# Attention's stages, the doubled global outputs and two casts issued at other places of a two-layer kernel

## The chip, the cores and the metric

One core of a Trainium2 chip runs the kernel. The metric is device time of one execution in microseconds (us); several runs are taken and their median is given. TensorE (PE) multiplies, VectorE (DVE), ScalarE (ACT) and GpSimd (POOL) do the elementwise work, SyncE (SP) issues every DMA here. Each engine runs its instructions in the order in which they were issued.

## The reference

Attention over 4 batches of 8 heads of 64, with 512 local and 32 global rows per batch. A local row attends to the global rows and to a window of 32 to each side; a global row attends to everything. The 2176 output rows of width 512 then go through two feed-forward layers (512 to 2048 to 512), all in float32:

```
s_g = scale * np.matmul(q_g, k_all.transpose(0, 1, 3, 2))
out_g = np.matmul(sm(s_g), v_all)
...
s_ll = np.where(mask, s_ll, -1000000000.0)
s_l = np.concatenate([s_lg, s_ll], axis=-1)
a_l = sm(s_l)
out_l = np.matmul(a_l, np.concatenate([v_g, v_l], axis=2))
...
h = x @ w_in
g = h * np.clip(h + 3.0, 0.0, 6.0) / 6.0          # first layer
g = np.where(h > 0.0, h, np.exp(np.minimum(h, 0.0)) - 1.0)   # second layer
(g @ w_out).astype(np.float32)
```

## The kernel before, in words

The rows are 17 tiles of 128: tiles 0 to 15 are local rows (four per batch), the last holds all the global rows. They are grouped into chunks 0 to 4 of 4, 3, 3, 3 and 4 tiles (`CHUNKS`). A chunk runs the first layer in 16 steps, one per block of 128 of the 2048 hidden columns (`f`). A matmul in float32 is done as three in a reduced format, of high and low parts (`xh`/`xl`, `gh`/`gl`), by `mm3`.

A step of the main loop issues, in this order: `up` (12 matmuls into `h`, then at once on ACT and DVE: `g` on ACT, `g` on DVE, `gh` on ACT), part 0's other work, `gl` on DVE, half of `down` (into `acc`) of the step two before, part 1's other work, the other half of `down`, part 2's other work. So a **place** is one of the three parts of a step; I write 5.2 for part 2 of step 5. Between parts 0 and 1 and between 1 and 2 PE has half a down step, between part 2 and the next step's part 0 a whole up.

While chunk 1 runs, attention of tiles 7 to 9 (chunk 2's) and of global blocks G0 to G2 is woven in; beside chunk 2 tiles 10 to 12 and G3 to G5, beside chunk 3 tiles 13 to 15, G6, G7 and the turning of the global outputs. (Chunk 0 has an order written out by hand, and tiles 4 to 6 are in it.) A local tile has four stages (`Local.stages`): scores **S** (64 small matmuls into two PSUM banks, then softmax on DVE and ACT, and the load of the next tile's q and k), **T** (8 transposes into two banks, two copies `PT` on ACT), values **O** (64 small matmuls into two banks, normalising on DVE, the load of the next v) and **XT** (4 transposes into one bank, then `x1h` on ACT and `x1l` on DVE, which read it: `split`). A global block has **SG**, **TG**, **OG** with `PG`, `PTG`, `xg` in the same roles. All of these share the two banks tagged `att`. At the end `turned_global` doubles four of the global outputs (`xgg`, a DVE copy of `xg`), transposes them (**XTG**) and splits the result; it runs twice.

The table `place, step` gives each stage a position, `during` stretches the positions of a chunk over 44 of its 48 places. Beside this `prepare`, a generator, splits the second layer's weights into high and low parts in eight passes and stores them to DRAM (`wd`). Each `yield` names the earliest place and what the next piece costs DVE and ACT; `Pace.step`, called behind each part's work, lets a piece go when its place has come and the work estimated for that engine stays under `ROOM`. Its pieces are `first` (L164), `second` (L167), `third` (L170 and L173), `high` (L179, a cast on ACT) and `low` (L183, on DVE).

Of the kernel before, what the change touches and what calls it, by code (L numbers as in the profile page):

```python
# [10 lines left out]
F32 = mybir.dt.float32  # L11
# [7 lines left out]
B, H, SL, SG, D = 4, 8, 512, 32, 64  # L19
# [4 lines left out]
P = 128  # L24
# [32 lines left out]
REBIAS = 2.0 ** -112  # L57


ROOM, FETCH, STORE = 2.25, 3, 4  # L60


def _tiles():
# [5 lines left out]
def tile_kernel(ctx, tc, qkW, vW, qkG, vN, vG, masks, w1, w2, out):  # L69
    nc = tc.nc  # L70
    pool = ctx.enter_context(tc.tile_pool(name="sb", bufs=1))
# [5 lines left out]
    NC = len(CHUNKS)  # L77
# [5 lines left out]
    xg = pool.tile([P, 2 * B, D], F32, name="xg")  # L83
    banks = {"acc": 4, "h": 2, "att": 2}

    def bank(shape, name, tag):
        return ps.tile(shape, F32, name=name, tag=tag, bufs=banks[tag])
# [65 lines left out]
    def prepare():  # L153

        def load(p, i, part, tag):
            raw = pool.tile([P, DM, 2], I32, name=f"raw1_{p}_{i}_{part}", tag=tag, bufs=1)
            src = w2[2 * p + i].bitcast(I32)[:, part * 2 * DM : (part + 1) * 2 * DM]
            nc.sync.dma_start(raw.rearrange("p c w -> p (c w)"), src)  # L160
            return raw

        def first(w, raw):
            nc.scalar.activation(w.bitcast(F32), raw[:, :, 1].bitcast(F32), AF.Copy, scale=REBIAS)  # L164

        def second(w):
            nc.vector.tensor_single_scalar(w, w, 3, op=ALU.logical_shift_left)  # L167

        def third(w, raw):
            nc.vector.scalar_tensor_tensor(  # L170
                w, raw[:, :, 1], -0x80000000, w, op0=ALU.bitwise_and, op1=ALU.bitwise_or
            )
            nc.vector.scalar_tensor_tensor(  # L173
                w, raw[:, :, 0], 29, w, op0=ALU.logical_shift_right, op1=ALU.bitwise_or
            )

        def high(src, n, name, tag):
            t = pool.tile([P, n, 2, DM // n], F32R, name=name, tag=tag, bufs=1)
            nc.scalar.copy(t[:, :, 0], src)  # L179
            return t  # L180

        def low(t, src):
            nc.vector.tensor_sub(t[:, :, 1], src, t[:, :, 0].bitcast(F32))  # L183

        def out(t, p, at):
            nc.sync.dma_start(wd[p][:, at * DM : at * DM + 2 * DM], t.bitcast(F32).rearrange("p n w k -> p (n w k)"))

        shaped = lambda w, n: w.bitcast(F32).rearrange("p (n k) -> p n k", n=n)
        A, B_, W, X = "f0", "f2", "f1", "f3"
        ra, rb = load(0, 0, 0, A), load(0, 1, 0, B_)  # L190
        ta = tb = pace.now
        for p in range(NF // 2):
            yield ta + FETCH, 0, 0.6
            w = pool.tile([P, 2, DM], I32, name=f"wi{p}", tag=W, bufs=1)
            wa, wb = w[:, 0], w[:, 1]
            first(wa, ra)
            yield pace.now + 1, 0.4, 0
            second(wa)
            yield 0, 1.4, 0
            third(wa, ra)  # L200
            yield tb + FETCH, 0, 0.6
            first(wb, rb)
            yield pace.now + 1, 0.4, 0.6
            ha = high(shaped(wa, 2), 2, f"ha{p}", A)
            second(wb)
            yield 0, 1.4, 0
            third(wb, rb)
            yield 0, 0.7, 0.6
            low(ha, shaped(wa, 2))
            la = pace.now  # L210
            hb = high(shaped(wb, 2), 2, f"hb{p}", B_)
            yield pace.now + 1, 0.7, 0
            low(hb, shaped(wb, 2))
            lb = pace.now
            yield 0, 0.8, 0
            sf = pool.tile([P, 4, 2 * P], F32, name=f"sf{p}", tag=X, bufs=1)
            half = lambda v, k: v.bitcast(F32)[:, 2 * P * k : 2 * P * k + 2 * P]
            nc.vector.tensor_add(sf[:, 2], half(wb, 0), half(wb, 1))
            nc.vector.tensor_sub(sf[:, 0], sf[:, 2], half(wa, 0))
            yield la + 2, 0, 0  # L220
            out(ha, p, 0)
            ta = pace.now
            yield 0, 0.8, 0
            nc.vector.tensor_sub(sf[:, 1], half(wa, 0), half(wb, 0))
            nc.vector.tensor_sub(sf[:, 3], half(wa, 1), sf[:, 0])
            tw = pace.now
            yield lb + 2, 0, 0
            out(hb, p, 2)
            tb = pace.now
            yield tw + 2, 0, 0  # L230
            oa = load(p, 0, 1, W)
            tw = pace.now
            yield ta + STORE, 0, 0.6
            s1 = high(sf[:, :2], 2, f"sa{p}", A)
            yield pace.now + 1, 0.7, 0
            low(s1, sf[:, :2])
            la = pace.now
            yield tb + STORE, 0, 0.6
            s2 = high(sf[:, 2:], 2, f"sb{p}", B_)
            yield pace.now + 1, 0.7, 0  # L240
            low(s2, sf[:, 2:])
            lb = pace.now
            yield la + 2, 0, 0
            out(s1, p, 8)
            ta = pace.now
            yield tw + FETCH, 0, 0.6
            w = pool.tile([P, 2, DM], I32, name=f"wo{p}", tag=X, bufs=1)
            wa, wb = w[:, 0], w[:, 1]
            first(wa, oa)
            yield lb + 2, 0, 0  # L250
            out(s2, p, 10)
            tb = pace.now
            yield 0, 0.4, 0
            second(wa)
            yield 0, 1.4, 0
            third(wa, oa)
            yield pace.now + 2, 0, 0
            ob = load(p, 1, 1, W)
            tw = pace.now
            yield ta + STORE, 0, 0.6  # L260
            ha = high(shaped(wa, 1), 1, f"oa{p}", A)
            yield pace.now + 1, 0.7, 0
            low(ha, shaped(wa, 1))
            la = pace.now
            yield tw + FETCH, 0, 0.6
            first(wb, ob)
            yield pace.now + 1, 0.4, 0
            second(wb)
            yield la + 2, 0, 0
            out(ha, p, 4)  # L270
            ta = pace.now
            yield 0, 1.4, 0
            third(wb, ob)
            tw = pace.now
            yield tb + STORE, 0, 0.6
            hb = high(shaped(wb, 1), 1, f"ob{p}", B_)
            yield pace.now + 1, 0.7, 0
            low(hb, shaped(wb, 1))
            lb = pace.now
            yield tw + 2, 0, 0  # L280
            if p + 1 < NF // 2:
                ra = load(p + 1, 0, 0, W)
            tw = pace.now
            yield lb + 2, 0, 0
            out(hb, p, 6)
            pace.done = p + 1
            yield ta + STORE, 0, 0
            if p + 1 < NF // 2:
                rb = load(p + 1, 1, 0, A)
            ta, tb = tw, pace.now  # L290
            A, B_, W, X = W, A, X, B_
# [25 lines left out]
    pace = Pace()  # L317
# [156 lines left out]
    class Global:  # L474
# [61 lines left out]
        def stages(self, nxt):  # L536
# [9 lines left out]

            return list(zip((first, self.transposed, third), ((1.0, 0.6), (0, 0.8), (0.9, 0))))

    def turned_global(hb):

        (xh, xl), c0 = x_of(len(tiles) - 1)
        xp = bank([P, 2, 2, 2, 2, SG], f"XTG{hb}", "att")
        twice = pool.tile([P, 4, 2, D], F32, name=f"xgg{hb}", tag="ev", bufs=4)
        nc.vector.tensor_copy(twice, xg[:, 4 * hb : 4 * hb + 4].unsqueeze(2).to_broadcast([P, 4, 2, D]))
        for i in range(4):
            transpose(
                xp[:, i // 2, i % 2].rearrange("p a r q -> p (a r q)"),
                twice[:, i].rearrange("p u d -> p (u d)"),
            )
        for par in range(2):  # L560
            r = slice(par * D, par * D + D)
            for b in range(2):
                cs = slice(c0 + (2 * hb + b) * SG, c0 + (2 * hb + b) * SG + SG)
                src = xp[r, b, :, :, par, :].rearrange("p h a q -> p (h a) q")
                nc.scalar.copy(xh[r, :, cs], src)
                nc.vector.tensor_sub(xl[r, :, cs], src, xh[r, :, cs].bitcast(F32))
# [338 lines left out]
    todo = {c: [] for c in range(NC)}  # L905
# [5 lines left out]
    at = {c: 0 for c in range(NC)}  # L911
    for (c, job), (_, nxt) in zip(jobs, jobs[1:] + [(None, None)]):
        if c is not None:
            place, step = ((0, 3, 5, 7), 9) if isinstance(job, Local) else ((0, 3, 5), 6)
            todo[c] += [(at[c] + x, st) for x, st in zip(place, job.stages(nxt=nxt))]
            at[c] += step
    todo[NC - 2] += [(at[NC - 2] + 3 + 2 * i, (lambda i=i: turned_global(i), (0.6, 0.6))) for i in range(2)]
    todo = {c: sorted(v, key=lambda x: x[0]) for c, v in todo.items()}

    def during(c, i):  # L920
# [170 lines left out]
```

## Time and profile before

| | us |
|---|---|
| median of 3 runs (864.95 to 866.28) | 864.99 |
| the profiled execution | 864.55 |
| its span | 862.8 |
| PE busy, 97% | 841.0 |
| DVE busy, 60% | 516.3 |
| ACT busy, 50% | 429.5 |

The span is the profiled stretch from the first to the last instruction; the execution's own time is a little longer. Busy counts modelled ends of pipelined matmuls, so two matmuls overlap in it. In the program's order chunk 1's first up begins at about 136 us, chunk 4's at 407 us.

### The profile page before, as it was taken

How to read it: one execution, taken by the hardware profiler on the slowest of the kernel's cores; microseconds unless marked ns; L12 is line 12 of the kernel's file. 1: busy time of each engine (PE TensorE's matmuls, PEld its weight loads, DVE VectorE, ACT ScalarE, POOL GpSimd, SP SyncE). 2: the span in 40 equal slices, each digit the busy share in tenths (PEclk: the TensorE clock that was granted, in tenths of full speed). 3: DMA queues.
4: the chain of work that ended last, by engine and by line, in shares of the span. 5: the costliest groups of instructions: out<-in, count | busy, mean ns of one | idle time of the engine just before them, and what ended most of it. 6: DMA issues, size and time to landing. Idle time of an engine off the chain costs nothing.

```text
span 862.8 us, 15804 instructions
## 1 busy us (share of the span) xinstructions
PE 841.0 (97%) x6424; PEld 727.1 (84%) x6424; DVE 516.3 (60%) x1125; ACT 429.5 (50%) x835; POOL 4.4 (1%) x8
## 2 busy tenths in 40 slices
PE   8899999999999999998999999999999999999997
PEld 7677778898988899887888889998998888888886
DVE  5788984666565556664655557444456665445443
ACT  6577655454544455543433346454445664444441
POOL 0000000000000000000000000000000000000000
PEclk9999999999999999999999999999999999999999
DMA  9958213656674765563589783946852656444102
GB/s 370 418 210 327 84 52 108 229 180 196 235 258 136 236 230 201 196 201 117 190 296 330 271 315 142 385 172 265 344 187 84 258 208 255 147 147 147 49 1 98
DMA packets 37657, 178.43 MB, mean 207 GB/s; under 512 B 4304, under 2 KB 6224, under 8 KB 25680
## 3 DMA queue, kind: packets, MB, share of 16 engines
q1 hardware_dynamic: 37584, 177.42, 56.9%
q8 instruction: 50, 0.82, 0.4%
q14 instruction: 23, 0.19, 0.1%
HBM read 143.33 MB, written 34.08 MB: 206 GB/s over the span
## 4 chain that ended last, share of the span: by engine, by line
PE 84%; DVE 7%; DMA 4%; ACT 3%; issue 2%; SPq 0%; ACTq 0%; DVEq 0%
PE acc L574 30%; PE h L574 22%; PE ua L574 9%; PE yt L574 9%; PE ub L574 7%; DMA v<-in_vW 1%; PE O L413 1%; PE S L381 1%; PE T L90 1%; DVE f L134 1%; DVE g L601 1%; DVE f L137 1%; DMA raw<-in_w 1%; DVE w L148 1%; DMA qk<-in_qkW 1%
## 5 line engine op out<-in xcount | busy, mean ns | idle before, releaser
L574 PE MATMUL acc<-gh,w 128*128 128x384 f32 (+1 forms) x640 | 199.5, 367 | 0.0
L574 PE MATMUL h<-x1h,w 128*128 128x384 f32 (+1 forms) x640 | 195.7, 367 | 1.6 <-DVE w L148 1.5
L574 PEld LDWEIGHTS h<-x1h,w 128*128 128x128 f32 x640 | 118.5, 189 | 20.1 <-issue 5.3
L574 PEld LDWEIGHTS acc<-gh,w 128*128 128x128 f32 x640 | 119.1, 189 | 13.4 <-issue 0.6
L574 PE MATMUL acc<-gl,w 128*128 128x384 f32 (+1 forms) x320 | 115.6, 361 | 0.8 <-DVE gl L608 0.8
L574 PE MATMUL h<-x1l,w 128*128 128x384 f32 (+1 forms) x320 | 115.5, 361 | 0.2 <-DVE x1l L445 0.2
L601 DVE SCALAR_TENSOR_TENSOR g<-g,h 128x384 f32<-128x384 f32 (+1 forms) x80 | 48.6, 607 | 110.4 <-ACT g L600 110.2
L600 ACT ACTIVATE g<-h,half 128x384 f32<-128x384 f32 (+1 forms) x80 | 49.8, 622 | 93.0 <-PE h L574 92.9
L606 ACT CAST gh<-g 128x384 fp32r<-128x384 f32 (+1 forms) x96 | 52.8, 550 | 77.0 <-DVE g L601 64.9
L574 PE MATMUL ua<-xs,ws 128*128 128x384 f32 (+1 forms) x384 | 88.0, 364 | 0.0
L574 PEld LDWEIGHTS ua<-xs,ws 128*128 128x128 f32 x384 | 70.4, 188 | 10.7 <-ACT s L835 0.3
L608 DVE TENSOR_TENSOR gl<-g,gh 128x384 fp32r<-128x384 f32 (+1 forms) x96 | 57.4, 599 | 24.6 <-ACT gh L606 24.1
L574 PEld LDWEIGHTS acc<-gl,w 128*128 128x128 f32 x320 | 60.4, 189 | 6.5 <-DVE gl L608 1.2
L574 PE MATMUL ub<-xs,ws 128*128 128x384 f32 (+1 forms) x288 | 65.7, 363 | 0.0
L574 PEld LDWEIGHTS h<-x1l,w 128*128 128x128 f32 x320 | 60.4, 189 | 6.1 <-DVE x1l L445 0.5
L574 PEld LDWEIGHTS ub<-xs,ws 128*128 128x128 f32 x288 | 52.7, 188 | 7.0
L877 DVE TENSOR_TENSOR y<-yt,y 128x512 f32<-128x512 f32 x49 | 33.8, 690 | 36.0 <-PE yt L574 35.5
L792 ACT ACTIVATE e<-c 128x384 f32<-128x384 f32 (+1 forms) x48 | 27.8, 580 | 45.8 <-DVE c L828 15.8
L574 PE MATMUL acc<-ws,gg_h 128*128 128x512 f32 x160 | 49.9, 393 | 0.0
L574 PE MATMUL yt<-ws,gg_h 128*128 128x512 f32 x160 | 49.9, 393 | 0.0
L795 DVE SCALAR_TENSOR_TENSOR e<-e,c 128x384 f32<-128x384 f32 (+1 forms) x48 | 30.0, 624 | 23.9 <-ACT e L793 23.3
L793 ACT ACTIVATE e<-e 128x384 f32<-128x384 f32 (+1 forms) x64 | 37.1, 579 | 2.0
(202 smaller groups left out, 1260.2 us busy)
## 6 DMA issues: line engine op xcount, KB each, us to landing
ws<-wd SPq DMA_DIRECT2D x48, 1024.0 KB, 5.4
raw<-in_w SPq DMA_DIRECT2D x16, 1024.0 KB, 11.7
raw<-in_w SPq DMA_DIRECT2D x32, 512.0 KB, 5.4
v<-in_vW SPq DMA_DIRECT2D x13, 1040.0 KB, 6.6
qk<-in_qkW SPq DMA_DIRECT2D x15, 704.0 KB, 6.0
qkG<-in_qkG SPq DMA_DIRECT2D x8, 608.0 KB, 4.6
wd<-ha SPq DMA_DIRECT2D x8, 512.0 KB, 4.8
wd<-hb SPq DMA_DIRECT2D x8, 512.0 KB, 4.8
```

What stands on the lines that cost most here:

```text
L90: nc.tensor.transpose(o, i, ident)
L134: nc.vector.scalar_tensor_tensor(w, self.high[:, s], -0x80000000, w, op0=ALU.bitwise_and, op1=ALU.bitwise_or)
L137: nc.vector.scalar_tensor_tensor(w, self.low[:, s], 29, w, op0=ALU.logical_shift_right, op1=ALU.bitwise_or)
L574: nc.tensor.matmul(o, a, b, start=first and i == 0, stop=last and i == len(pairs) - 1, skip_group_check=more)
L600: nc.scalar.activation(g, hp, AF.Relu, scale=1.0 / 6.0, bias=half)
L601: nc.vector.scalar_tensor_tensor(g, g, 1.0, hp, op0=ALU.min, op1=ALU.mult)
L606: nc.scalar.copy(gh, g)
L608: return lambda: nc.vector.tensor_sub(gl, g, gh.bitcast(F32))
L792: nc.scalar.activation(e, h, AF.Relu, scale=-1.0)
L793: nc.scalar.activation(e, e, AF.Exp, scale=-1.0)
L795: 1, lambda: nc.vector.scalar_tensor_tensor(e, e, -1.0, h, op0=ALU.add, op1=ALU.max)
L877: nc.vector.tensor_add(y, o, y)
```

## The change

Seven edits in the part that orders the work; each instruction stays as it is.

```diff
-ROOM, FETCH, STORE = 2.25, 3, 4
+ROOM, FETCH, STORE = 2.4, 3, 4
...
             third(wb, rb)
-            yield 0, 0.7, 0.6
+            yield pace.now + 1, 0.7, 0.6
             low(ha, shaped(wa, 2))
             la = pace.now
             hb = high(shaped(wb, 2), 2, f"hb{p}", B_)
...
             tw = pace.now
-            yield tb + STORE, 0, 0.6
+            yield max(tb + STORE, tw + 1), 0, 0.6
             hb = high(shaped(wb, 1), 1, f"ob{p}", B_)
...
+    xgg = {}
+
+    def doubled(hb):
+        xgg[hb] = pool.tile([P, 4, 2, D], F32, name=f"xgg{hb}", tag="ev", bufs=4)
+        nc.vector.tensor_copy(xgg[hb], xg[:, 4 * hb : 4 * hb + 4].unsqueeze(2).to_broadcast([P, 4, 2, D]))
+
...
-        xp = bank([P, 2, 2, 2, 2, SG], f"XTG{hb}", "att")
-        twice = pool.tile([P, 4, 2, D], F32, name=f"xgg{hb}", tag="ev", bufs=4)
-        nc.vector.tensor_copy(twice, xg[:, 4 * hb : 4 * hb + 4].unsqueeze(2).to_broadcast([P, 4, 2, D]))
+        xp, twice = bank([P, 2, 2, 2, 2, SG], f"XTG{hb}", "att"), xgg.pop(hb)
...
-            place, step = ((0, 3, 5, 7), 9) if isinstance(job, Local) else ((0, 3, 5), 6)
+            place, step = ((0, 4, 5, 7.5), 9.5) if isinstance(job, Local) else ((0, 2, 4), 5)
...
-    todo[NC - 2] += [(at[NC - 2] + 3 + 2 * i, (lambda i=i: turned_global(i), (0.6, 0.6))) for i in range(2)]
+    todo[NC - 2] += [(at[NC - 2] + 2 * i, (lambda i=i: doubled(i), (0.6, 0))) for i in range(2)]
+    todo[NC - 2] += [(at[NC - 2] + 2 + 3 * i, (lambda i=i: turned_global(i), (0.6, 0.6))) for i in range(2)]
```

Worked out from the table, the stages stand at these places (before, then after):

| | S or SG | T or TG | O or OG | XT |
|---|---|---|---|---|
| tiles 7, 10 | 0.0, 0.0 | 0.2, 1.1 | 1.1, 1.2 | 2.0, 2.1 |
| tiles 8, 11 | 2.2, 3.0 | 3.2, 4.1 | 4.1, 4.2 | 5.0, 5.2 |
| tiles 9, 12 | 5.2, 6.1 | 6.2, 7.2 | 7.1, 8.0 | 8.0, 8.2 |
| tile 13 | 0.0, 0.0 | 0.2, 1.0 | 1.1, 1.1 | 2.0, 2.1 |
| tile 14 | 2.2, 3.0 | 3.2, 4.1 | 4.1, 4.2 | 5.0, 5.1 |
| tile 15 | 5.2, 6.0 | 6.2, 7.1 | 7.1, 7.2 | 8.0, 8.2 |
| G0, G3, G6 | 8.2, 9.1 | 9.2, 10.0 | 10.1, 10.2 | |
| G1, G4, G7 | 10.2, 11.0 | 11.2, 11.2 | 12.1, 12.1 | |
| G2, G5 | 12.2, 12.2 | 13.2, 13.1 | 14.1, 14.0 | |

The two XTG stand at 13.2 and 14.1 before, at 13.1 and 14.1 now; the copies `xgg` stood in the same places and are now at 12.2 and 13.1. A step of prepare moves by at most two places.

The order on DVE at the end of chunk 3 (`g0_3_13` is g of layer 0, chunk 3, step 13; `oa`, `wo` are prepare's), before:

```order
L534 TENSOR_SCALAR xg_67<-OG7_4869,sumG7_4774 128x64
L601 SCALAR_TENSOR_TENSOR g0_3_13_4916<-g0_3_13_4916,h0_3_13_4903 128x384
L183 TENSOR_TENSOR oa4_4901<-wo4_4820,oa4_4901 128x512
L608 TENSOR_TENSOR gl0_3_13_4918<-g0_3_13_4916,gh0_3_13_4917 128x384
L554 COPY xgg0_4938<-xg_67 128x512
L566 TENSOR_TENSOR x1l4_4156<-XTG0_4937,x1h4_4155 64x4x32 x4
L167 TENSOR_SCALAR wo4_4820<-wo4_4820 128x512
L601 SCALAR_TENSOR_TENSOR g0_3_14_4967<-g0_3_14_4967,h0_3_14_4954 128x384
L170 SCALAR_TENSOR_TENSOR wo4_4820<-raw1_4_1_1_4893,wo4_4820 128x512
L173 SCALAR_TENSOR_TENSOR wo4_4820<-raw1_4_1_1_4893,wo4_4820 128x512
L608 TENSOR_TENSOR gl0_3_14_4969<-g0_3_14_4967,gh0_3_14_4968 128x384
L554 COPY xgg1_4985<-xg_67 128x512
```

and with the change:

```order
L534 TENSOR_SCALAR xg_67<-OG7_4869,sumG7_4794 128x64
L553 COPY xgg0_4899<-xg_67 128x512
L605 SCALAR_TENSOR_TENSOR g0_3_13_4918<-g0_3_13_4918,h0_3_13_4905 128x384
L183 TENSOR_TENSOR oa4_4903<-wo4_4820,oa4_4903 128x512
L612 TENSOR_TENSOR gl0_3_13_4920<-g0_3_13_4918,gh0_3_13_4919 128x384
L553 COPY xgg1_4932<-xg_67 128x512
L570 TENSOR_TENSOR x1l4_4167<-XTG0_4934,x1h4_4166 64x4x32 x4
L605 SCALAR_TENSOR_TENSOR g0_3_14_4967<-g0_3_14_4967,h0_3_14_4954 128x384
L167 TENSOR_SCALAR wo4_4820<-wo4_4820 128x512
L170 SCALAR_TENSOR_TENSOR wo4_4820<-raw1_4_1_1_4901,wo4_4820 128x512
L173 SCALAR_TENSOR_TENSOR wo4_4820<-raw1_4_1_1_4901,wo4_4820 128x512
L612 TENSOR_TENSOR gl0_3_14_4969<-g0_3_14_4967,gh0_3_14_4968 128x384
```

The copy xgg0 has moved from behind g, oa and gl of step 13 to straight behind the last xg, and xgg1 from behind the whole of step 14 to the place ahead of XTG0's x1l.

ACT at the start of chunk 3 (`P13` is softmax's exp of tile 13, `PT13` the copies behind its T), before:

```order
L394 ACTIVATE P13_3953<-P13_3953,mn13_3957 128x128 x8
L403 COPY PT13_3954<-T13_0_4023 128x512
L403 COPY PT13_3954<-T13_1_4029 128x512
L179 CAST sa3_4035<-sf3_3914 128x2x256
L600 ACTIVATE g0_3_1_4050<-h0_3_1_4037,half_65 128x384
L606 CAST gh0_3_1_4051<-g0_3_1_4050 128x384
L179 CAST sb3_4057<-sf3_3914 128x2x256
```

and with the change:

```order
L394 ACTIVATE P13_3952<-P13_3952,mn13_3956 128x128 x8
L604 ACTIVATE g0_3_1_4036<-h0_3_1_4023,half_65 128x384
L610 CAST gh0_3_1_4037<-g0_3_1_4036 128x384
L403 COPY PT13_3953<-T13_0_4042 128x512
L403 COPY PT13_3953<-T13_1_4048 128x512
L179 CAST sa3_4054<-sf3_3921 128x2x256
L642 COPY ev0_2_0_4060<-acc0_2_0_3003 128x384
```

Tile 13's two PT copies have moved behind g and gh of step 1.

ACT in steps 8 to 11 of chunk 3 (`x1h4` is read from tile 15's XT; `PG6`, `PG7` are the exps of G6 and G7), before:

```order
L444 CAST x1h4_4155<-XT15_4616 128x4x128
L179 CAST hb4_4631<-wi4_4492 128x2x256
L510 ACTIVATE PG6_4639,sumG6_4641<-PG6_4639,mnG6_4640 128x544
L600 ACTIVATE g0_3_9_4672<-h0_3_9_4659,half_65 128x384
L606 CAST gh0_3_9_4673<-g0_3_9_4672 128x384
L520 COPY PTG6_4698<-TG6_4700 128x512
L523 COPY PTg6_4699<-Tg6_4706 32x128
L600 ACTIVATE g0_3_10_4722<-h0_3_10_4709,half_65 128x384
L606 CAST gh0_3_10_4723<-g0_3_10_4722 128x384
L179 CAST sa4_4764<-sf4_4678 128x2x256
L510 ACTIVATE PG7_4772,sumG7_4774<-PG7_4772,mnG7_4773 128x544
L179 CAST sb4_4790<-sf4_4678 128x2x256
```

and with the change:

```order
L444 CAST x1h4_4166<-XT15_4632 128x4x128
L604 ACTIVATE g0_3_9_4653<-h0_3_9_4640,half_65 128x384
L610 CAST gh0_3_9_4654<-g0_3_9_4653 128x384
L510 ACTIVATE PG6_4670,sumG6_4672<-PG6_4670,mnG6_4671 128x544
L604 ACTIVATE g0_3_10_4711<-h0_3_10_4698,half_65 128x384
L610 CAST gh0_3_10_4712<-g0_3_10_4711 128x384
L520 COPY PTG6_4717<-TG6_4719 128x512
L523 COPY PTg6_4718<-Tg6_4725 32x128
L179 CAST sa4_4737<-sf4_4659 128x2x256
L604 ACTIVATE g0_3_11_4786<-h0_3_11_4773,half_65 128x384
L610 CAST gh0_3_11_4787<-g0_3_11_4786 128x384
L510 ACTIVATE PG7_4792,sumG7_4794<-PG7_4792,mnG7_4793 128x544
```

Between x1h of tile 15 and the exp of G6 a step's g and gh now stand, and the exp of G7 has moved behind g and gh of step 11.

## Rows read from the trace of the kernel before

**Rows 1.** The page, busy time of each engine.
```profile
PE 841.0 (97%) x6424; PEld 727.1 (84%) x6424; DVE 516.3 (60%) x1125; ACT 429.5 (50%) x835; POOL 4.4 (1%) x8
```
**Rows 2.** Waits of PE: who waited for whom, us in total, times, longest.
```profile
PE XTG L90 <- DVE xgg L554: 3.3, 2, 2.6
PE S L381 <- DVE x1l L445: 2.7, 4, 1.7
...
PE OG L531 <- ACT PTG L520: 0.6, 1, 0.6
```
**Rows 3.** Timeline of PE at S: start, us, line, operation; idle time before it.
```profile
153.66 0.40 PE L381 MATMUL S<-qk 64*32 64x128 f32 x2
...
155.35 0.45 PE L574 MATMUL h<-x1h,w 128*128 128x384 f32 x1
...
317.17 1.16 PE L381 MATMUL S<-qk 64*32 64x128 f32 x64
318.25 0.44 PE L574 MATMUL acc<-gh,w 128*128 128x384 f32 x1
...
348.87 0.40 PE L381 MATMUL S<-qk 64*32 64x128 f32 x2
349.85 1.14 PE L381 MATMUL S<-qk 64*32 64x128 f32 x62 [0.57 <-DVE x1l L445]
350.92 0.44 PE L574 MATMUL h<-x1h,w 128*128 128x384 f32 x1
```
**Rows 4.** Timeline of PE at SG.
```profile
187.59 1.31 PE L503 MATMUL SG<-qkG 64*32 64x272 f32 x16
188.83 0.44 PE L574 MATMUL h<-x1h,w 128*128 128x384 f32 x1
...
199.00 0.74 PE L503 MATMUL SG<-qkG 64*32 64x272 f32 x16
199.66 0.44 PE L574 MATMUL h<-x1h,w 128*128 128x384 f32 x1
```
**Rows 5.** Timelines of PE, ACT and DVE around the XT of tile 7.
```profile
151.04 0.60 PE L90 MATMUL XT<-ident,x 128*128 128x128 f32 x4
151.39 0.42 PE L574 MATMUL acc<-gh,w 128*128 128x384 f32 x1
...
152.93 0.58 ACT L444 CAST x1h<-XT 128x512 fp32r<-128x512 f32 x1
...
151.93 0.55 DVE L601 SCALAR_TENSOR_TENSOR g<-g,h 128x384 f32<-128x384 f32 x1
153.54 0.69 DVE L445 TENSOR_TENSOR x1l<-XT,x1h 128x512 fp32r<-128x512 f32 x1 [1.06 <-ACT x1h L444]
```
**Rows 6.** The chain that ended last, in chunk 3: start, us, what.
```profile
313.07 2.08 PE acc L574 x12
```
**Rows 7.** Timelines of PE and DVE at the second XTG.
```profile
396.94 0.34 PE L574 MATMUL acc<-gh,w 128*128 128x384 f32 x1
399.87 0.84 PE L90 MATMUL XTG<-ident,xgg 128*128 128x128 f32 x4 [2.59 <-DVE xgg L554]
...
399.30 0.42 DVE L554 COPY xgg<-xg 128x512 f32<-128x512 f32 x1
```
**Rows 8.** Windows: us, busy of PE, PEld, DVE, ACT, POOL, granted clock, DMA.
```profile
400.00:404.00 4.00, 4.00 (x16) 4.00 (x16) 1.84 (x5) 1.04 (x4) 0.00 (x0) 0.57 0.40 127
```
**Rows 9.** Timelines of DVE and ACT behind an SG, its first PG operation and exp.
```profile
199.81 0.44 DVE L505 TENSOR_SCALAR_CACHE_REDUCE PG<-SG 128x272 f32<-128x272 f32 x1 [0.82 <-PE SG L503]
...
200.91 0.75 ACT L510 ACTIVATE PG<-PG,mnG 128x544 f32<-128x544 f32 x1 [3.16 <-DVE mnG L509]
```
**Rows 10.** Waits of ACT.
```profile
ACT wi L164 <- DMA raw<-in_w: 2.8, 1, 2.8
```
**Rows 11.** Tile qkG's loads, and the longest store wait of SP's queue (chunks 1 to 3).
```profile
DMA to landing us min/median/max: 4.0/4.6/5.5
...
SPq L186 <- DVE oa L183: 6.9, 1, 6.9
```

## The prediction

> **What bounds the kernel now.** I read the page first: TensorE (PE) is busy 841.0 of 862.8 us [rows 1], so what a new order can give is a part of 21.8 us of idle time plus what the pipelining hides. The view of PE's waits names the idle time: in chunks 1 to 3 it is S waiting for x1l, XTG waiting for xgg and one OG waiting for PTG, 6.6 us together [rows 2]. The chunks 0 and 4 and the whole second layer are not touched.
>
> Then the timeline of PE, by starts and not by idle columns. A block S that waits for nothing takes 1.08 us to the next start (317.17 to 318.25). The first S that is held takes 1.69 (153.66 to 155.35), the last 2.05 (348.87 to 350.92) [rows 3]; the four between take 1.69, 3.15, 1.60 and 1.60. Over 1.08 each, the six lose 0.61 + 0.61 + 2.07 + 0.52 + 0.52 + 0.97 = 5.30 us. SG likewise: 0.66 free, 1.24 held [rows 4]; with two more of 1.23 and 1.19 that is 1.68 us.
>
> These nine have one cause. Every second S (or SG) bank is freed by the x1l of the XT two places earlier. XT stood in part 0 of a step, right behind the step's own up; on ACT its x1h comes behind that step's g and gh, and starts 1.89 us after XT (151.04 to 152.93); x1l ends at 154.23, 3.19 after XT [rows 5]. PE needs the bank after XT (0.35) and two halves of a down step. A whole down step is 2.08 us [rows 6], as is an up of the same twelve matmuls, a half 1.04: 2.43 in all. It is short by up to 0.76, however idle DVE is.
>
> XTG waits for a copy that is issued in the same place: the first loses 0.7 [rows 2]. The second starts 2.93 after the matmul before it where 0.17 is the rule, so 2.76, of which the idle column shows 2.59; the copy began at 399.30 behind work of prepare [rows 7]. [...]
>
> **The change, part by part.** No engine gets or loses an instruction; queues are permuted, POOL's not at all.
>
> *XT to the next S or SG.* Now XT stands in part 1 or 2, and an up lies between it and the next S. From the start of XT PE has at least 0.35 + 2.08 + 1.04 = 3.47 us. XT in part 1 comes 1.04 later in its step, so gh is past 0.85 after XT and x1l ends 3.19 - 1.04 = 2.15 after it. For tiles 7, 10 and 14 two integer operations of prepare, about as long as x1l's 0.69 (the same 512 columns), now stand ahead of x1l on DVE: some 3.0 by 3.47. Still no wait. Bounds: all 5.30 + 1.68 = 7.0 us gained, or nothing. I take 7.0, because the margin is positive in each of the nine.
>
> *XTG.* xgg0 now runs straight behind the last xg, one g and one gl ahead of its XTG; xgg1 a whole step ahead. Gain 0.7 + 2.76 = 3.5 us. Next late would be the att bank or x1h; the bank was freed by G7 a step earlier, and x1h and x1l of XTG gate only chunk 4's first up. [...]
>
> *OG of G5*: it waited 0.6 [rows 2] since two first steps of prepare, the second held by its load, stood ahead of PTG on ACT. They now stand behind it: 0.6. Two T's that lose 0.2 to 0.3 are left out.
>
> *T to O, now one place.* For eight of nine tiles T stands in part 1 or 2. With T in part 1 ACT is past gh at 1.89 - 1.04 = 0.85 after T; a PT copy takes what x1h takes, 0.58 [rows 5], and ends at 1.43, while PE comes to O after the eight transposes (twice XT's 0.35) and a half step, 1.74. No wait. Tile 13 is the exception: its T is in part 0, so PT starts at 1.89 and ends at 2.47, against 1.74: **a new wait of 0.7**.
>
> *SG to TG of G1, G4, G7, from three places to two.* SG is now in part 0. DVE must first run g, which ends 1.44 after the step's start (151.93 + 0.55 - 151.04) [rows 5]; from the first PG operation to exp it is 1.10, and exp takes 0.75 [rows 9]: 3.29. PE comes to TG after SG 0.66 and two halves: 2.74. **A new wait of 0.55 three times, 1.65.** G0, G3, G6 keep an up between SG and TG, and G2, G5 too.
>
> *O to XT*: for tiles 9 and 12 both halves of a step instead of a half and an up. Normalising has to be done in 2.08 us after O; no wait before shows its need, and I take none; if it came out as long as the wait of tile 13 it would be 2 x 0.7.
>
> *ROOM and the two later casts* move prepare's steps by at most two places either way. Nothing on PE waits for prepare before the second layer, and it ends in the same place as before. The cover is the slack of ACT and DVE; if it is gone, a cast of about 0.6 in front of PT or exp would show in full. Its loads keep at least three places to the step that reads them. On SP, x2d stores pass a load of v, and stores and raw loads pass loads of qkG and vN, by one or two rows.
>
> Sum: 5.30 + 1.68 + 3.46 + 1.7 + 0.6 = 12.74 gained, 0.7 + 1.65 = 2.35 given back, **10.4 us net**. Against the profiled execution's 864.55 (its span and 1.75 around it) that is 854.15; the median of the runs is 0.44 higher, so **854.6 us**.
>
> By the idle column alone the S, XTG and OG waits are 6.6 us, and the sum would be 6.6 + 1.7 - 2.35 = 5.95, or 859.0. The last held S decides: idle 0.57, lost 0.97 [rows 3]. [...]
>
> **The rivals.**
> 1. *The clock still falls once*, at another wait. [...] 854.6 + 1.7 = 856.3. 8%.
> 2. *A moved load is late and ACT stands still in front of a PT or an exp.* For it: ACT has waited 2.8 us for a raw tile once [rows 10], and the loads now meet other traffic. Against: once in eight passes, and then PE lost 0.6. Two such waits that reach PE whole: 854.6 + 5.6 = 860.2. 12%, anywhere between.
> 3. *The spacing doesn't do what it says*: x1l stays last because prepare's operations slide in ahead of it with XT. Then the 7.0 stay and 3.4 is left: 861.6. For it: three tiles have these operations ahead now. 6%.
> 4. *Slower: global loads too late.* SG follows SG after five places instead of six. qkG has one buffer, is issued when the SG before has been read, and lands in 4.0 to 5.5 us [rows 11]. From G1 to G2 the cover is SG 0.66 and 6.24 of matmuls, 6.9 (TG and OG come on top); 0.66 + 5.5 = 6.2 leaves 0.7. If SP held the load behind another queue entry as long as the 6.9 that one store waited [rows 11], five SGs would lose 6.2 each: 31 - 10.4 = 21 over before, 886. It decides from a hold of 0.7 + 10.4 / 5 = 2.8 us on each. Against: no wait of an SG for a load in the kernel before, and what stands ahead of those loads in the new order is stores of tiles made two places earlier. 4%; a mild form, near no change, 3%.
>
> **How the numbers follow.** The forecast as summed, with new waits anywhere between none (852.2; the two T's make it 851.8) and those named, has 67%. The range from 851.8 to 860.2 takes in rivals 1 and 2 and leaves out rivals 3 and 4. About 0.2%, 1.7 us, is what a measurement of this kernel tells from no change: faster by more 0.93 (67 + 8 + 12 + 6), within 0.03, slower 0.04.
>
> **What would show it.** Right: PE's waits have no row of S or SG on x1l and none of XTG on xgg; the granted clock is 1.00 from chunk 1 to 4; S takes 1.1 to the next start everywhere. New rows: one O on PT of about 0.3 to 0.7, TG on exp three times about 0.2 to 0.5 (the idle column shows less than is lost). Chunk 4 and all behind it as long as before. Wrong: x1l rows still there (rival 3), SG on qkG (rival 4), a stretch at the lower clock (rival 1), or more than 2.4 us of new waits of O, XT or TG.

## The result, and the profile after

The changed kernel takes **851.45 us** (median of 4 runs, 850.82 to 851.54), the kernel before 865.08 beside it (4 runs, 864.95 to 866.28): ratio 0.984, interval 0.9824 to 0.9856. That is 13.6 us faster where 10.4 were forecast, and 0.35 below the low end of the range. A second series gave 852.1 (4 runs, 851.57 to 852.95) against 863.67: ratio 0.9864, interval 0.9848 to 0.9881. The profiled execution took 851.54, span 849.8.

The page, busy time of each engine, after (for [rows 1]):

```profile
PE 835.3 (98%) x6424; PEld 724.5 (85%) x6424; DVE 514.7 (61%) x1125; ACT 430.2 (51%) x835; POOL 4.4 (1%) x8
```

PE is idle for 14.5 us, where it was 21.8. Waits of PE in the trace after, chunks 1 to 3: who waited for whom, us in total, times, longest (for [rows 2]):

```profile
PE TG L90 <- ACT PG L510: 1.2, 3, 0.7
PE O L413 <- ACT PT L403: 0.4, 1, 0.4
```

All old rows are gone: no S waits for x1l, no XTG for xgg, no OG for PTG. What is left are the four new waits that were forecast. Timeline of PE after, at the S of tile 15 and at the SG of G1 (for [rows 3, 4]):

```profile
345.71 1.16 PE L381 MATMUL S<-qk 64*32 64x128 f32 x64
346.79 0.44 PE L578 MATMUL acc<-gh,w 128*128 128x384 f32 x1
...
199.24 0.69 PE L503 MATMUL SG<-qkG 64*32 64x272 f32 x16
199.86 0.45 PE L578 MATMUL acc<-gh,w 128*128 128x384 f32 x1
```

S takes 1.08 to the next start (2.05 in the last held one before), SG 0.62 (1.24 when held). All nine S and all eight SG read so. Timeline of PE at the second XTG, and a window over it: us, busy of the engines, granted clock (for [rows 7, 8]):

```profile
389.56 0.34 PE L578 MATMUL acc<-gh,w 128*128 128x384 f32 x1
389.74 0.60 PE L90 MATMUL XTG<-ident,xgg 128*128 128x128 f32 x4
...
389.00:394.00 5.00, 5.00 (x33) 4.96 (x31) 3.30 (x8) 2.12 (x6) 0.00 (x0) 1.00 0.12 27
```

XTG starts 0.18 after the matmul before it (2.93 before), and the granted clock is 1.00 over these 5 us. The second XTG has come forward from 399.87 to 389.74, chunk 4's first up from 407.18 to 395.38.

The new waits, timelines of PE and ACT after, at the TG of G1 and at the O of tile 13 (for [rows 9]):

```profile
201.88 0.34 PE L578 MATMUL acc<-gh,w 128*128 128x384 f32 x1
202.87 0.66 PE L90 MATMUL TG<-ident,PG 128*128 128x128 f32 x4 [0.65 <-ACT PG L510]
...
199.10 0.81 ACT L164 ACTIVATE wi<-raw 128x512 f32<-128x512 f32 x1 [2.55 <-DMA raw<-in_w]
199.82 0.56 ACT L604 ACTIVATE g<-h,half 128x384 f32<-128x384 f32 x1
...
201.98 0.75 ACT L510 ACTIVATE PG<-PG,mnG 128x544 f32<-128x544 f32 x1 [0.46 <-DVE mnG L509]
...
319.47 0.34 PE L578 MATMUL acc<-gh,w 128*128 128x384 f32 x1
320.23 1.16 PE L413 MATMUL O<-v,PT 128*32 128x65 f32 x64 [0.43 <-ACT PT L403]
...
319.18 0.51 ACT L610 CAST gh<-g 128x384 fp32r<-128x384 f32 x1 [0.62 <-DVE g L605]
319.60 1.07 ACT L403 COPY PT<-T 128x512 f32<-128x512 f32 x2
```

TG of G1 starts 0.99 after the matmul before it where 0.17 is the rule, so 0.82 are lost; G4 loses 0.43 and G7 0.42, together 1.67. The 0.4 that G1 loses over the others come from a load: ACT waits 2.55 us for a raw tile, and its g starts 0.58 after SG (199.24, 199.82), which is 0.17 at G4 (286.05, 286.22). O of tile 13 starts 0.76 after where 0.27 is usual: 0.49, since both PT copies stand behind gh. Waits of ACT, and the landing of the loads of qkG (for [rows 10, 11]):

```profile
ACT wi L164 <- DMA raw<-in_w: 9.4, 6, 2.7
...
DMA to landing us min/median/max: 3.5/5.1/6.8
```

ACT waits for a raw tile six times instead of once; one of the six is the wait ahead of G1's exp, the others show in no row of PE. Loads of qkG take up to 6.8 and no SG waits for them. So rival 2 came in small, at 0.4 us, and rival 4 found its traffic but no price.

**Where the 13.0 us between the two profiled executions (864.55 and 851.54) come from.** Chunk 1's first S is 0.22 earlier (137.91, 137.69): the start of the kernel, untouched, where the traces spread from 137.47 to 138.24 (e9, at a mean clock of 0.996, 139.12). From there to chunk 4's first up 11.58. From that up to the last group of acc nothing: 444.91 before (852.09 - 407.18), 444.87 after (840.25 - 395.38). And 1.16 behind that, at the very end: from the start of the last copy on DVE to the end of the span it is 4.95 before (862.8 - 857.85), 3.79 after (849.8 - 846.01).

### The profile page after: what moved, and what is told of

Its sections match the earlier page's. It is cut to its first block, busy times and chain, and to the rows that moved or that the text cites. A ratio compares the mean times of both kernels' runs of the same rounds, so it can differ in the third digit from the quotient of the medians.

```text
span 849.8 us, 15802 instructions
## 1 busy us (share of the span) xinstructions
PE 835.3 (98%) x6424; PEld 724.5 (85%) x6424; DVE 514.7 (61%) x1125; ACT 430.2 (51%) x835; POOL 4.4 (1%) x8
## 4 chain that ended last, share of the span: by engine, by line
PE 88%; DVE 5%; DMA 3%; ACT 2%; issue 1%; SPq 0%; ACTq 0%
PE acc L578 33%; PE h L578 23%; PE ua L578 9%; PE yt L578 9%; PE ub L578 7%; PE O L413 2%; DMA v<-in_vW 1%; PE S L381 1%; DVE f L134 1%; PE T L90 1%; DVE f L137 1%; DMA raw<-in_w 1%; DMA qk<-in_qkW 1%; DVE w L148 1%; PE XT L90 1%
```

## The experiments

The kernel before beside them took 864.76 (7 runs, e1 to e4), 864.85 (17 runs, 862.27 to 867.32, e5 to e8) and 863.67 (7 runs, the last two).

### Which part of the change gives what (e1, e2, e3)

**e1: the new places alone** (XTG's too, the copy still inside it).

```diff
-            place, step = ((0, 3, 5, 7), 9) if isinstance(job, Local) else ((0, 3, 5), 6)
+            place, step = ((0, 4, 5, 7.5), 9.5) if isinstance(job, Local) else ((0, 2, 4), 5)
...
-    todo[NC - 2] += [(at[NC - 2] + 3 + 2 * i, (lambda i=i: turned_global(i), (0.6, 0.6))) for i in range(2)]
+    todo[NC - 2] += [(at[NC - 2] + 2 + 3 * i, (lambda i=i: turned_global(i), (0.6, 0.6))) for i in range(2)]
```

> Only the stages' places (and those of the two XTG) are the changed kernel's; the doubling copy stays in XTG's own place, prepare's casts and ROOM stay as before. Theory 'places': the held S and SG go by their places alone (no wait of S or SG on x1l), and the new waits (tile 13's O, TG of G1, G4, G7) come. XTG0 now meets a whole third of prepare and gl ahead of its copy: some 3.2 us of wait, XTG1 some 1.9, together 5.1, and the clock falls once (1.7). So 851.45 + 5.1 + 1.7 = 858.2, between 856.5 and 860. Theory 'prepare': with the old ROOM and casts, x1l stays behind prepare's operations and at least half of the S and SG waits stay: 861 to 865.

Measured 861.84 (860.24 to 862.28), ratio 0.9957 (0.994 to 0.9974). Waits of PE in its trace, chunks 1 to 3:

```profile
PE XTG L90 <- DVE xgg L554: 4.6, 2, 2.8
PE TG L90 <- ACT PG L510: 1.0, 4, 0.4
PE SG L503 <- DVE xg L534: 0.5, 1, 0.5
PE O L413 <- ACT PT L403: 0.4, 1, 0.4
```

No S waits for x1l: the spacing does what the forecast said, and rival 3 is out. But the time lies 3.6 us over the 858.2 expected, in the range of theory 'prepare', whose S waits did not stay. XTG waits 4.6 where it waited 3.3 before, about as expected (3.15 and 2.12 from the matmul before, 4.9 lost by starts). What the expectation lacked: SG of G2 and G5 lose 0.65 and 1.11 by starts, behind xg; the end is 1.16 longer, and chunk 4 with the rest takes 0.7 more (both below).

**e2: the doubling copies alone**, moved ahead of XTG.

```diff
-        twice = pool.tile([P, 4, 2, D], F32, name=f"xgg{hb}", tag="ev", bufs=4)
-        nc.vector.tensor_copy(twice, xg[:, 4 * hb : 4 * hb + 4].unsqueeze(2).to_broadcast([P, 4, 2, D]))
...
+    todo[NC - 2] += [(at[NC - 2] + 2 * i, (lambda i=i: doubled(i), (0.6, 0))) for i in range(2)]
```

> Only the doubling copies are moved (to 12.2 and 13.1; XTG stays at 13.2 and 14.1), all else as before. Theory 'places': the two XTG waits (0.88 + 2.76) and the fall of the clock (1.7) go, the S and SG waits stay: 865.1 - 5.3 = 859.8 (859.2 to 860.4). If the clock's fall has another cause: 861.5.

Measured 859.43 (858.24 to 859.89), ratio 0.9931 (0.9915 to 0.9947). XTG waits no more. That makes 0.88 + 2.76 for XTG and 1.7 for the clock at that place; yet in this trace the clock falls elsewhere. Timeline of PE at the S of tile 11 in e2 (it waits for the x1l of tile 10), and windows over it, first of e2, then of the kernel before:

```profile
241.39 0.40 PE L381 MATMUL S<-qk 64*32 64x128 f32 x2
243.48 1.24 PE L381 MATMUL S<-qk 64*32 64x128 f32 x62 [1.69 <-DVE x1l L445]
...
244.00:248.00 4.00, 4.00 (x56) 3.71 (x41) 2.27 (x17) 2.45 (x8) 0.00 (x0) 0.57 0.94 272
```
```profile
244.00:248.00 4.00, 4.00 (x76) 3.80 (x57) 2.47 (x18) 2.75 (x9) 0.00 (x0) 1.00 0.93 261
```

The same wait is in both kernels (1.69 here, 1.68 before). In e2 a granted clock of 0.57 on average over 4 us follows, and PE gets through 56 instructions where it was 76; in the trace before it stays at 1.00. So the 859.8 expected came out, but not by the working behind it: the fall was not removed, it moved, and the end stayed long. In its place the OG of G5 waits no more (0.65), though nothing of prepare is changed: the raw load ahead of PTG lands at the same time (307.73, before 307.67), and PE comes to that OG later (309.47; before 308.86 with the wait in it).

**e3: prepare's edits alone**, `ROOM` and the two casts.

```diff
-ROOM, FETCH, STORE = 2.25, 3, 4
+ROOM, FETCH, STORE = 2.4, 3, 4
-            yield 0, 0.7, 0.6
+            yield pace.now + 1, 0.7, 0.6
-            yield tb + STORE, 0, 0.6
+            yield max(tb + STORE, tw + 1), 0, 0.6
```

> Only ROOM and the two later casts are changed. Theory 'places': no wait of PE hangs on them, 865.1 within 1 us, all S, SG and XTG waits still there. Theory 'prepare': at least a third of the gain, 860.5 or less.

Measured 859.69 (859.43 to 859.87), ratio 0.9936 (0.9921 to 0.995): 5.1 us from the edits that the forecast priced at nothing. Its waits of PE:

```profile
PE XTG L90 <- DVE xgg L554: 3.3, 2, 2.6
PE S L381 <- DVE x1l L445: 1.2, 5, 0.4
```

XTG as before, but S waits 1.2 instead of 2.7, and the OG row is gone. The timelines of ACT at tile 10's x1h tell why, before and then in e3:

```profile
240.18 0.62 ACT L179 CAST ob<-wo 128x512 fp32r<-128x512 f32 x1 [3.20 <-DVE wo L173]
240.71 0.58 ACT L600 ACTIVATE g<-h,half 128x384 f32<-128x384 f32 x1
241.91 0.51 ACT L606 CAST gh<-g 128x384 fp32r<-128x384 f32 x1 [0.62 <-DVE g L601]
242.32 0.58 ACT L444 CAST x1h<-XT 128x512 fp32r<-128x512 f32 x1
```
```profile
238.94 0.58 ACT L600 ACTIVATE g<-h,half 128x384 f32<-128x384 f32 x1 [2.23 <-PE h L574]
240.39 0.51 ACT L606 CAST gh<-g 128x384 fp32r<-128x384 f32 x1 [0.87 <-DVE g L601]
240.81 0.58 ACT L444 CAST x1h<-XT 128x512 fp32r<-128x512 f32 x1
241.29 0.62 ACT L179 CAST ob<-wo 128x512 fp32r<-128x512 f32 x1
```

Before, a cast of prepare stood on ACT ahead of g, gh and x1h, and ACT idled 3.20 us in front of it until DVE had made its input. Issued one place later it stands behind x1h, which now starts 2.13 us after XT (238.68) and not 3.37 (238.95). S's second bank comes 0.84 after its first (241.33, 242.17) where it came 2.08 after (241.60, 243.68): 1.24 gained of the 2.07 that this S, tile 11's, loses. At tile 14's x1h such a cast stood ahead too, behind 2.98 us of idle time, and S of tile 15 gains 0.35. With OG's 0.65, which is gone here too (as it is in e2 without these edits), that is 2.24. The rest of e3's gain is the short end (3.76 in its trace) and the clock: behind the same idle 2.59 us at XTG it does not fall. Timeline of PE and a window, e3:

```profile
397.23 0.63 PE L90 MATMUL XTG<-ident,xgg 128*128 128x128 f32 x4 [2.59 <-DVE xgg L554]
...
397.00:402.00 5.00, 4.77 (x29) 4.80 (x30) 2.18 (x7) 2.25 (x6) 0.00 (x0) 1.00 0.33 105
```

The four runs of e3 all have a mean clock of 0.999 over the span.

### Casts or ROOM (e6, e7)

The two expectations name the waits after other tiles: their S of tile 10 is tile 11's, behind tile 10's x1l, and their tile 12 is S of tile 15.

```diff
-            yield 0, 0.7, 0.6
+            yield pace.now + 1, 0.7, 0.6
-            yield tb + STORE, 0, 0.6
+            yield max(tb + STORE, tw + 1), 0, 0.6
```

> The kernel before with the two later casts alone. Theory: at tile 10 a cast of prepare stands on ACT ahead of g and x1h and waits 3.20 us for its third step; moved behind x1h, S of tile 10 loses 0.8 instead of 2.1 (1.2 us gained), OG of G5 waits no more (0.65), tile 12 0.35: 862.7 us with one fall of the clock, 861.0 with none, 1.1 less with the short end. If ROOM was what moved them: as before, 864.8.

```diff
-ROOM, FETCH, STORE = 2.25, 3, 4
+ROOM, FETCH, STORE = 2.4, 3, 4
```

> The kernel before with ROOM 2.4 alone. Theory: ROOM leaves the cast of tile 10 ahead of g and x1h and the raw load ahead of PTG of G5, so S of tile 10 loses 2.1 and OG 0.65 as before: 864.8 us, less up to 1.7 if the clock does not fall and 1.1 if the end is the short one. If ROOM is what helped: 862.7 or less, with the wait of S of tile 10 below 0.8.

The casts alone: 860.67 (859.64 to 861.86, 8 runs), ratio 0.9957 (0.9942 to 0.9972). `ROOM` alone: 865.86 (863.32 to 867.87, 10 runs), ratio 1.0004 (0.9988 to 1.0021). The waits of PE in e6 read as in e3. Those in e7:

```profile
PE XTG L90 <- DVE xgg L554: 4.3, 2, 2.6
PE S L381 <- DVE x1l L445: 2.8, 5, 1.7
PE OG L531 <- ACT PTG L520: 0.7, 1, 0.7
```

It is the casts; `ROOM` alone leaves S, OG and XTG waiting. (e6 came out lower than 862.7 and 861.0 because its end is the short one, as the expectation allowed; e7 is 1 us over the 864.8 expected, with XTG waiting 1.0 us more.) That they and the places do the same work at tile 10's x1l is why the parts cannot be added: each takes the wait of that S away by itself. The gains alone, 2.9 (e1), 5.3 (e2) and 5.1 (e3), come to 13.3 of the 13.6 only by chance: in e1 XTG loses 1.3 more than before and two SG wait, and the OG wait is counted more than once.

### Do prepare's edits still matter beside the rest (e5)

The changed kernel with `ROOM` and both casts put back.

> The changed kernel with ROOM and the two casts of prepare back as they were; new places and doubled copies stay. If the new places by themselves already keep prepare's casts out of the way of x1h (with the places alone no S waited, and chunks 1 to 3 lost about 2.0 us against the changed kernel ahead of the first XTG), 853.5 us, or 854.6 with the long end of the program. If the 5.1 us that prepare's edits gave alone were independent of the places: 851.45 + 5.1 = 856.5. If prepare did nothing, 851.5.

Measured 854.76 (854.64 to 855.06), ratio 0.9886 (0.9863 to 0.991): the first theory, with the long end. Its chunk 4 begins at 397.32, 1.94 later than after the whole change, and its end is 1.16 longer. PE's waits are those of e1 without the XTG row. By starts SG of G2 and G5 lose 0.66 and 1.11 of the 1.94. Timelines of DVE and PE at the SG of G5, e5:

```profile
295.14 0.69 DVE L173 SCALAR_TENSOR_TENSOR wo<-raw,wo 128x512 int32<-128x512 int32 x1
296.67 0.28 DVE L534 TENSOR_SCALAR xg<-OG,sumG 128x64 f32<-128x64 f32 x1
...
297.01 0.69 PE L503 MATMUL SG<-qkG 64*32 64x272 f32 x14 [0.47 <-DVE xg L534]
```

A third step of prepare stands on DVE ahead of the xg that frees the bank, and xg starts 0.77 behind the SG (295.90). After the whole change no such step is there, and xg starts 0.36 ahead of it (294.89, 295.25). So beside the new places prepare's edits take away another wait than they do alone.

### Does an idle time of that length lower the clock (e4, and the kernel once more)

e4 is the changed kernel with the second copy back inside XTG's place.

```diff
-    todo[NC - 2] += [(at[NC - 2] + 2 * i, (lambda i=i: doubled(i), (0.6, 0))) for i in range(2)]
+    todo[NC - 2] += [(at[NC - 2] + 5 * i, (lambda i=i: doubled(i), (0.6, 0))) for i in range(2)]
```

> The changed kernel with the second doubling copy back in the place of its XTG (14.1). The copy then stands behind a third of prepare and gl: XTG1 waits some 3.4 us. If the fall of the granted clock hangs on PE's long idle time there, it falls behind it and costs 1.7 more: 851.45 + 3.4 + 1.7 = 856.6. If the fall in the kernel before was chance or had another cause: 854.9 with the clock at 1.00.

Measured 856.77 (854.96 to 857.43), ratio 0.9905 (0.9886 to 0.9923). Both cases occur: the profiled run took 854.96 with no fall, the other three 856.13 to 857.43 at a mean clock of 0.996 to 0.998. Timeline and window of the profiled one:

```profile
392.33 0.63 PE L90 MATMUL XTG<-ident,xgg 128*128 128x128 f32 x4 [3.02 <-DVE xgg L553]
...
392.00:397.00 5.00, 4.67 (x28) 4.70 (x29) 2.18 (x7) 2.25 (x6) 0.00 (x0) 1.00 0.31 105
```

> The changed kernel once more. If the clock does not fall in it because no idle time is long enough, every run reads 1.00 or 0.999 and lies between 850.8 and 851.6 us, and the end behind the last copy on DVE is the short one again (3.8 us). If the absence of the fall was luck, some runs are 1.7 us longer.

Measured 852.1 (851.57 to 852.95); all four runs have a mean clock of 0.999 or 1.00, the end is short again (3.8 us). One fall of 1.7 us would take 0.002 off the mean. With the first series that is eight runs of the changed kernel without a fall. Three of the four lie over the upper bound expected. In the profiled one 0.55 of the 0.61 us over the first series' lie ahead of chunk 1's first S (138.24, 137.69), where nothing was changed; why is open.

### Two tries for the waits that are left (e8, e9)

e8: second global block of each chunk one place later, and T and O of tile 13; e9: tile 13 alone.

```diff
-            place, step = ((0, 4, 5, 7.5), 9.5) if isinstance(job, Local) else ((0, 2, 4), 5)
+            place, step = ((0, 4.1, 5.1, 7.5), 9.5) if isinstance(job, Local) else ((0, 2, 4), 5)
...
+            late = 1 if job in globs[1::3] else 0
-            todo[c] += [(at[c] + x, st) for x, st in zip(place, job.stages(nxt=nxt))]
+            todo[c] += [(at[c] + late + x, st) for x, st in zip(place, job.stages(nxt=nxt))]
```

> The changed kernel with the second global block of each chunk one place later (SG in part 1, not 0) and T and O of tile 13 one place later. If the new waits are what the places make them, all four go: TG 1.67 + 0.18 behind it, O 0.49, in all 2.3 us: 849.1. If the global loads, which have one place less to G2 and G5, land too late, SG waits for qkG instead and the time is 851.5 or more.

> The changed kernel with T and O of tile 13 one place later, all else alike. If the new wait of O is what its place makes it, O of tile 13 is 0.10 late as every other O and the time is 0.5 us shorter than that of the changed kernel beside it: 850.9. If O one place later delays its XT and the next S instead, the same time or longer, and S of tile 14 waits for x1l.

e8: 854.81 (853.97 to 856.08), against 851.45 and 852.1 for the changed kernel in the two other series; its traced waits are longer too. Waits of PE, and the timeline of PE at the SG of G2, e8:

```profile
PE SG L503 <- DVE xg L534: 2.6, 2, 1.6
PE O L413 <- ACT PT L403: 1.2, 3, 0.6
...
207.52 0.31 PE L531 MATMUL OG<-vN,PTg 32*32 32x64 f32 x8
207.76 0.64 PE L503 MATMUL SG<-qkG 64*32 64x272 f32 x2
209.47 0.69 PE L503 MATMUL SG<-qkG 64*32 64x272 f32 x14 [1.07 <-DVE xg L534]
```

TG waits no more, but the SG behind OG in the same place needs the bank that xg still reads: G2 and G5 lose 1.71 and 2.22 by starts, and three O together 1.4, where the four waits of the changed kernel lost 2.2. (In the profiled run, the slowest, the clock also falls once, behind the SG of G5.) e9: 851.9 (851.57 to 853.4), against 852.1 for the changed kernel beside it: no difference that can be told. In its profiled run PT stands on ACT behind an `sa` cast and a copy `ev`, and O loses more than after the change, 1.37 instead of 0.49 (timeline of PE, e9):

```profile
323.10 1.10 PE L413 MATMUL O<-v,PT 128*32 128x65 f32 x60 [1.30 <-ACT PT L403]
```

(That run, 853.4, is the longest of the four, at a mean granted clock of 0.996; the other three had 0.998 to 1.000.) No version tried beats the changed kernel.

## Why the prediction was right in its mechanism and which steps failed

- **Right: the mechanism and the sign.** XT's place set the wait of S and SG, and with the new places none of the nine waits (in e1, without prepare's edits, no S does either): x1l now ends 1.95 to 2.79 us after XT, where the prediction had 2.15 to 3.0 against the 3.47 that PE gives. The starts were the right measure: by the idle column the sum was 859.0. PE's idle time on the page fell by 7.3 us where the time fell by 13.0; its busy time fell by 5.7 [rows 1] with the same 6424 matmuls. That starts show the loss rests on the rows here (0.57 idle, 0.97 lost).
- **Right: the new waits.** TG 1.67 against 1.65, O 0.49 against 0.7, together 2.16 against 2.35. That TG fits so closely is luck: by its place a TG loses 0.42, and the late load at G1 adds 0.4.
- **Mis-sized: the middle, 11.6 against 10.4.** "Two T's that lose 0.2 to 0.3 left out" were 0.48 and came whole. The first XTG lost 0.88 by starts (393.44 against the matmul before it), not the 0.7 of the idle column: the rule of measuring by starts was not kept there. OG was 0.65, and the SG of G5 had lost 0.2 (299.27, 0.85 to the next start) that was not counted. With the 0.19 of new waits that did not come this is 1.1 of the 1.2.
- **Failed: "Nothing on PE waits for prepare".** S of tile 11 and 15 and the OG of G5 did, through ACT's order: 2.24 us in e3's trace. One cause was named for nine waits, and there were two; the prediction's own rows said so, since XT's place is short by up to 0.76 and those two S lose 2.07 and 0.97. The same waits were booked under the places and the OG term, so these did little harm to the sum. But the edits themselves were put at nothing, and without them the changed kernel takes 3.1 us more in the traces (e5, 854.76 by median): 1.94 up to chunk 4, as SG of G2 and G5 wait for an xg behind prepare, and 1.16 at the end.
- **Failed: "Chunk 4 and all behind it as long as before".** The end became 1.16 us shorter. Without this, or without the 1.2 of the middle, the result would lie inside the range; so would the second series (852.1) as it is. DMA queues from the last store's issue to the end, kernel before and then the changed one:

```profile
q1 hardware_dynamic: 179, 0.30, 23.3%
q14 instruction: 1, 0.01, 0.6%
...
out<-ev SPq DMA_DIRECT2D x1, 256.0 KB, 3.2
```
```profile
q1 hardware_dynamic: 188, 0.32, 26.7%
...
out<-ev SPq DMA_DIRECT2D x1, 256.0 KB, 2.0
```

  Before, one packet of the queue q14 (instruction), 0.01 MB, goes in this stretch, and the last store lands in 3.2 us instead of 2.0. The traces of e1, e2 and e5 have packet and 3.2 as well, and a long end of 4.9; e3 has neither. The four kernels without any of prepare's edits have the long end in their traces (4.9); of those with some of them the traces of the changed kernel (both), e3, e4 and e9 have the short one, 3.72 to 3.79. That the packet holds the store up is argued from this, not tried by itself, and why those edits move it is open.
- **The clock** was booked at 1.7 for one fall, as it stood in the profiled execution: 0.43 of the 4 us at 0.57 [rows 8]. That the fall would go with the long idle time was the author's estimate and no run shows it: idle times of 2.59 us (e3) and 3.02 us (e4) went by at 1.00. It never fell in the changed kernel, so the term came whole; but in the kernel before it is a matter of the run (below), and a median of that kernel holds what its runs happened to meet.

## What to carry to other kernels

Ask of every side task what stands behind it on its engine when its input is late: a cast that costs 0.6 us kept ACT idle for 3.2, and x1h behind it came 1.24 us later to PE's cost. Book all waits by starts, the small ones too, and try the parts of a change alone before adding them up, because two edits can remove the same wait. A wait on TensorE can cost more than itself: behind 1.69 us of idle time in e2 and 2.59 in the kernel before the granted clock read 0.57 over 4 us, some 1.7 us more (0.43 of 4).

## What the runs showed of the hardware

- **The length of an idle time did not decide whether the clock falls.** After idle times of 1.69 us (e2) and 2.59 us (before, [rows 7, 8]) the granted clock read 0.57 on average over 4 us, and 0.50 from 400.5 to 403.5 us of the kernel before; 0.43 of 4 us is 1.7 us lost. After 1.68 (before, S of tile 11), 2.59 (e3) and 3.02 (e4) it stayed at 1.00. Some idle time was there each time: in the twelve traces, from chunk 1 to the last matmul, PE is idle for 1.58 us or more twelve times, a fall follows within 1.5 us in seven of them, and no fall is elsewhere. The 17 runs of the kernel before in one series had mean clocks from 0.993 to 0.998 and took 862.27 to 867.32 us; the 8 of the changed kernel 0.999 to 1.000. What sets the clock no run here shows.
- **A packet of the instruction queue near the end of the last store went with 1.2 us more**: 3.2 us to landing in the four traces that have it there (before, e1, e2, e5), 2.0 in those of the changed kernel and e3, which have none in that stretch.
- **TensorE's tempo was not one at a granted clock of 1.00.** From chunk 4's first up to the last group of acc the traces of before, after, e2, e5, e8 and e9 take 444.9 us (the second of the changed kernel 445.0), those of e1, e3, e4 and e6 445.6 (e3: 848.58 - 403.00), with the same matmuls; e7 takes 446.6. These five had waited at an XTG for 2.6 to 3.0 us, but so had the kernel before, which has the quicker tempo. What decides is open.
